# One tile for q and k of a head pair, wider scores matmuls, and part of VectorE's copies and of the gate's "+1" on GpSimd: an attention + gated FFN kernel on one Trainium2 core

## The chip, the cores and the metric

The kernel runs on one core of one Trainium2 chip. The core has five engines that run side by side, each through its own instructions in order: TensorE (PE in the profile; its weight loads are shown apart as PEld), VectorE (DVE), ScalarE (ACT), GpSimd (POOL) and SyncE (SP, which here only issues DMAs). The metric is the device time of one execution in microseconds (us); the number to predict is the median over runs. A profile is one execution with a record of every instruction.

## What is computed

Block-sparse attention (8 heads of 64, 4 batches, 768 tokens) and behind it a feed-forward network with a gate that is a convolution over three neighbouring tokens. In the reference's words, cut to what matters (B, H, S, D = 4, 8, 768, 64):

```python
scores = np.matmul(q, k.transpose(0, 1, 3, 2)) / np.sqrt(D)
...
scores = np.where(mask, scores, -1000000000.0)   # blocks of 32: window, edges, 3 sampled per row
attn = np.exp(scores - np.max(scores, axis=-1, keepdims=True))
attn = attn / (np.sum(attn, axis=-1, keepdims=True) + 1e-09)
x = np.matmul(attn, v).transpose(0, 2, 1, 3).reshape(B, S, H * D)
...
h = np.maximum(x @ w_in, 0.0)                    # 512 -> 1024
for k in range(3):
    conv_out += conv_w[k] * hp[:, k:k + S, :]    # hp: h with one zero row at each end
gate = 1.0 / (1.0 + np.exp(-conv_out))
out = (h * gate) @ w_out                         # 1024 -> 512
```

## The kernel before

The work is cut into 144 units of 1024 scores columns, in segments: half a batch (384 query tokens) each, the last half again in 256 + 128. Two heads form a pair; there are 16 pairs. A unit goes through this chain:

- *Scores* (L742, PE). For a 128-key block `kc` and a head, the stationary operand is k transposed, 88 rows: 64 of k and 24 rows that carry the block mask. The moving operand is q transposed with the mask's other factor in its 24 rows, so that the masked scores come out of one matmul. The result goes to a PSUM tile `st` of 1024 columns. There are two of these.
- *Exponential* (L753, ACT): one instruction for a unit, 128x1024, from `st` to `pt` in SBUF.
- *Attention times v* (L775, PE): eight matmuls of 65 columns for a unit; the 65th column of `V_t` is ones, so that the sums come along. DVE then takes reciprocals (L692) and normalises (L694), and the tokens are transposed into `xT`.
- *Feed-forward*: w_in matmuls (L864, PE), relu (L884 on ACT or L886 on DVE), the three-tap convolution as three DVE multiplies and two adds (L916, L924), tanh (L963, ACT), "+1" (L966, DVE), product with h (L971, DVE, to `gT`), w_out matmuls (L802, PE), copy from PSUM to `o2s` (helper lines L336 on ACT, L340 on DVE), output DMA (L809, SP).

q and k of a pair lie in two tiles, `E_t` and `O_t`, by the parity of the 128-token chunk: `E` has k chunks 0, 2, 4 and three of the six q chunks, `O` the rest. For pairs 0 to 5 they come from PE transposes (k: L466; q: L504, three 64-column ones for a head and half) and copies from PSUM; for pairs 6 to 15 from DMA transposes into `stg` and one DVE copy for each parity. The mask rows are made once in slot 0 and copied by DVE into the other four slots (`m_slot`, two copies of 1536 for each slot). v comes by DMA into `vn` and is copied into `V_t` with room for the ones column (`v_cp`, by DVE or ACT). The tap weights as diagonal matrices (`diag`, L387, DVE) serve the last segment, whose convolution is done on PE.

Since the q chunks of one half lie in both tiles, a scores matmul of one k block covers 128 or 256 columns (`blk_order`, `pieces`):

```python
blk_order = {0: [(0, 0, 0), (0, 1, 2), (1, 0, 1)], 1: [(1, 1, 0), (1, 2, 2), (0, 2, 1)]}
...
if pieces and pieces[-1][:4] == (P, hh, kc, par) and pieces[-1][4] + pieces[-1][6] == idx:
    pieces[-1] = pieces[-1][:6] + (pieces[-1][6] + 1,)
```

What sets the order: each piece of work is an `op` with the engines that may do it and a planned duration for each, its dependencies and buffers. A string, `ORDER`, written beforehand, lists all 1758 in one sequence with the engine and the buffer number of each; `put_down` walks it. So each engine's order is fixed, and an engine waits at an instruction whose data isn't there, with all behind it. Semaphores are placed by the framework, tile by tile.

POOL before: at the start it builds index tables (`affine_select`, L265 to L275), then it issues all loads of q, k, v and weights (L239, 65 of them), held back by 43 `pace` copies of one element (L414, L656), which only wait until an exponential or an earlier load is done.

The last two output blocks (`tail`) accumulate in the two halves of one `st` tile.

Of the kernel before, what the change touches and what calls it, by code (L numbers as in the profile page):

```python
# [8 lines left out]
BF16 = mybir.dt.bfloat16  # L9
# [23 lines left out]
i+18Y4i/2MV8/090j0Vj109158r2941958sj22Uj71960j3V9909a8Mjm0j409b12+9h1jo2/08t29i8Njnj89j2j58O0jp9m09nj9V8U0j6A8V
319r1jq9o3ja1jbju1jd0jvjrje8P9s9w0jcAjx8Z321308+92jfA93jwjj19t49xjC2jg0jhjyiZ9y5369E1js372jkjiV9798jz9cjE9F2u0jD
9d19G09J0jA9k9KjF9l9L19e19O1jt9p9q339PjlV9u2wA9T02vAjB9U9vk819Q2jK3k9jL9z9V3jGjY0393a29Y19f9A9ZjHjMa409g9H09IjN
9M9+4jZjOa59N9R8QjI9SjP9W3c9XjJa91aaa65kajQiT9/jRj+3bab09B2ae09Cj/2VV3af9Dk0A2kb3h2WVaj1ag1k20a11a2k33d0kcA3k4
2ZA3k5jS1k6V1a30jT34V4akjUal2ar0k1jVa01asjWA0ke0kfat3jXkh1kgV1kiaw135V3kkjAax3l3kn0ay4kokC03i0kk1kEaB0kpAklkDaC
kmAa7kFa8acaG1aD5kq0kGadaHkK1kt1kH3nahkMaL0kr3o13mkLaI0aikuksVamaMkvAkNkz03eaN1aT1kOaUkw1kS2ankPkx3skIkAao0kTaY0
aV2aZkJ1au0avazaAkyVaEkBAaFaJb11kVa+3b2aKkQl61apaOb34b60kRaqb7lc0kUb85be1k+3bfl7l03pbg0aP1kWaWbj0bkaQ2aXk/kXa/b0
b4bo1aRb5b9bl1bal1aSbh0bpldkYl2bq2bt0bikZbubmbb1l3lebcby1bzbv3bdl4bnl8l5brbsbA43qV0bG0bHk7l938V43fV1bI5lf3v3w1  # L40
laV2bL1bMlgA0bwbQ03rVli1bN0lh3gVljll0kdlkV3jA0lm3AbRlblnVbV1bWbS1lr1lG0lo0lIlsbX23x3B1lplHc10c2ltV3t1lqAbxc61lJ
c33c7bBbC1lO1lx1lylKc84cb0bJlzVcclD0lLlQcg1bKlP3ychlu1cd5bD0lRbObPlvbEbTci0lElMcl0bF1lSbUcmlwAbY3KlNct13L0lTlA1
lW2bZculYcn1c40lB3zlXc5c9calFVcv33Hcy03I2czb+2lUcelZlCAmg03PlVcA4cD1cfcEl+mh3Mb/cF2cjcI0ck3uV1ma1c0m23l/cJcom3
cp1cQ1cRcK5m4cw3CcxcBm5cCcGmbcS0m0m6cV0cHcLm1cM3NcWm7c+1cq1micrcX1c/m8mccscN0m9cT0cUd03d30cOd4mjcPd54cY3Zmd3+2
mkV1d81d9meV0mm03Q0da5dg03DV2mn3JV2mo3EV423OcZmfdhd1mpdi03W3Gdl1mqV3dmmy1dn1mz3/mB0mC3X0mAA0dq0mDVd2drms1mW0ds2
mtmX3Rdv1dwmYmudx3mZmE0mv40m+431d6d7mwV2mFm/dD0dbmGVdEdI1dc1n0dF4mH1n10mIdJdd2mJAmN04cde4d3dN0dK5mOn21df2dj41dO
n3dkmK1n4dP0mL494a1n5domxdpdS1dTmPVmMA4hdtdudX0dU13SV3dYdy3TVmQ1mRdZ2n6e314e4i0e4na2dzmT0nbe53mUmSVdG0e80dHe9n7
mVVdLed1dA1eeni3ea4nw1dBdMdQdRncdVef5dCdWd+ei04fndejnq0n8ek0e00eq1neer3Fd/1n9e6e744es1ev0njewnrnkex3eA1e1eb3VeB
ecnlege2nfehel4gem3YV3et0eF0nmeC4nx4ong4p2eueyen2eznheGnneK1eonyeH5eLepnonsnpeDeEeM045V4eS0eT4jnteU2eX1nuV0eYnz
eZ14bV4eI48eJnAV2eNf00mrf1eO1eP1f5146Vf23mlf6nC0eQ47nDf74nI1eR0nEVnJfd04qV0nKAfe4kV1nL0ff5nM3Ufi1nNVnvfjnF14lV  # L50
fk0eV4nnGo60eWnBfn0fonHAo8nR0fp2nSo7fs1n+1e+e/ftnTAn/nO1fu1nPo9fx0o0fyf3nQAf4o1nU0fz3fF1oafGf8f9o2nVfH4nX1oe2fg0
fK0offLo3nYogfhfP1fa0fM5flnZVfQfmfqo4frfbobfU0o5fvfcfVnWAohoA1fR0ocfwou0om3fAodfW2g01g1onfB1fIovoig21g50oog6oBop
ojfJfNfC2fOoqfSg73fTga1fDgbfXfYokfEg30org4g8olg9gj0gkgc4osoCotowgl5fZ1go1f+gpoxgq0f/gdoDoyV3gt0gugeoM0gv24mgf0oN
ggozoOoEA1oPoFgC1oQA0gDgh1gH0giA1gIoS0gE1oToV1oUV1gJ3oWgM1oXVgNp20gO4p3pe1p51pgp6p4Apfgm1gV0p7AgngrphoY0oZpigW
o+Agso/1pu0pjp0pwoG0pvp1Ag+1g/gX5oHpm2oIpnh00oJpogwh30pph4oKA2gxpxpb1h52gF0pqoLpcp80gy2pkoRgGpdAgKgzgLgPhc1prpy
hdgQpl1gY1gZhe1h1p9psh2gR1h6ptgA1hh0paAh7gShigBAhq1h80pC3hrhj3pK0pDgT1pLh9hs4gUVhf0hz0pFhgha1hkpzhl1hbVhApEhthu
pZ1hB5hv2pGp+hwhE1pHp/VhFhN0hC1hOpAhG0q31pIpBq4pJhDpMq5Aqe1hHpNhP2hJ1hm0pQ1qfhnpRpOA3qhpSqu2ho0qgpThpA2qwhI0pW0
pUA1hKqvpXpVqihL1hQhRpYAhMVpPhS0hx1hThyAq60qjhU0q01hVVq7qR0qSq8q1qTAq9qkq2AqO0qaqPqlr31qbqX1qQVqYr4qcq+0qZAqU0qd
qVq/qm3qC1qWAqor01qDqnr50qI0r1r6r80r2rd1qpri0qqr9rer7ro1qrqxrprf1qyra0qJqsqzqtrjqEqAqBqKrbqLrcrgqFrhqMA2rqqGV0qN
rrrkqHrsA1rlrtrmA3rn  # L60
# [52 lines left out]
def kernel(  # L113
# [23 lines left out]
    WHOLE = ()  # L137
    SEQ = "nq0 nq1 k4 q4 w0 v4 w1 nq2 w2 k5 q5 w3 v5 nq3 k6 q6 v6 k7 q7 v7 nq4 nq5"
# [16 lines left out]
    E_t = many(NSLOT, [88, 2, 2, 3, 128], BF16, "e")  # L155
    O_t = many(NSLOT, [88, 2, 2, 3, 128], BF16, "o")
# [145 lines left out]

    ECH, OCH = [(0, 0), (0, 2), (1, 1)], [(0, 1), (1, 0), (1, 2)]

    def w24(e):
        w = st_t[b_w.index]
        for x, chunks in enumerate((ECH, OCH)):
            for y, (g, c) in enumerate(chunks):
                nc.tensor.matmul(out=w[0:NB, 512 * x + 128 * y:512 * x + 128 * y + 128], lhsT=aadd,
                                 rhs=nblk[:, 384 * g:384 * g + 384].rearrange("j (p c) -> j c p", c=3)[:, c],  # L310
                                 start=True, stop=True)

    o_w = op("w24", {"PE": 0.34}, w24, -17, [o_a4, o_nblk], alloc=[b_w])

    def q_rows(dst, x):
        def fn(e):
            w = st_t[b_w.index][0:NB, 512 * x:512 * x + 384]
            to = dst[64:88, 0, 0].rearrange("p c s -> p (c s)")
            if e == "ACT":
                nc.scalar.copy(out=to, in_=w)  # L320
            else:
                nc.vector.tensor_copy(out=to, in_=w)
        return fn

    m_q = [op("m_q0", {"ACT": 0.45, "DVE": 0.55}, q_rows(E_t[0], 0), -17, [o_w], uses=[b_w]),
           op("m_q1", {"DVE": 0.55, "ACT": 0.45}, q_rows(O_t[0], 1), -17, [o_w], uses=[b_w])]

    def k_rows(dst, x):
        return lambda e: dcopy(e, dst[64:88, 1, 0], nblk.rearrange("j (p c t) -> j t c p", c=3, t=2)[:, x])

    m_k = [op("m_k", {"DVE": 0.6, "ACT": 0.5}, k_rows((E_t, O_t)[x][0], x), -13, [o_nblk]) for x in range(2)]
    mask_ready = {(0, 0): m_q + m_k}

# [12 lines left out]
    def wl(e):  # L346
        for y, (t0, c, n_) in enumerate(((384, 0, 2), (640, 0, 1), (384, 1, 2))):
# [7 lines left out]
    m_h1 = []  # L355
    for x, t in enumerate((E_t, O_t)):
        m_h1.append(op("m_h1", {"DVE": t_d4(768)}, lambda e, t=t: dcopy(e, t[0][64:88, :, 1], t[0][64:88, :, 0]),
                       T(0) + 0.1 * x, [m_q[x], m_k[x]]))
    mask_ready[(0, 1)] = m_h1
    for s in range(1, NSLOT):  # L360
        mr = []
        for x, t in enumerate((E_t, O_t)):
            mr.append(op("m_slot", {"DVE": t_d4(1536) + 0.05}, lambda e, t=t, s=s: dcopy(e, t[s][64:88], t[0][64:88]),
                         T(4.5 * s - 2.5) + 0.1 * x, [m_h1[x]], earliest=7.0 + 2 * s))
        mask_ready[(s, 0)] = mask_ready[(s, 1)] = mr
# [354 lines left out]
    for u, (n, blocks) in enumerate(units):  # L720
# [3 lines left out]
        for part in range(2):  # L724
            bls = blocks[4 * part:4 * part + 4]
            heads, pieces = [], []
            for x, (P, hh, kc, par, idx, c) in enumerate(bls):
                if (P, hh) not in heads:
                    heads.append((P, hh))
# [288 lines left out]
```

## Time and profile before

| what | us |
|---|---|
| runs | 217.66, 217.71, 220.73 |
| median | 217.71 |
| the profiled execution's own time | 215.81 |
| its span, first to last instruction | 213.9 |
| first exponential starts | 7.88 |
| last evicting copy ends | 210.9 |

The page gives for each engine the time in which at least one of its instructions was running (busy). Records of consecutive instructions overlap by their latency, so a busy engine need not be at its peak: for the rate, compare starts. The chain that ended last is followed back from the last instruction, at each step to what released it; its shares say on which engine time is on the path. A group's line reads: line, engine, operation, output<-inputs, shapes, count | busy us, mean ns of one | idle time before them and what ended it. A timeline's line: start, duration, engine, line, operation, tiles, shape, count [idle before <- releaser].

The TensorE clock was at its full value in the whole profile (PEclk 9, the highest digit, in all slices).

### The profile page before, as it was taken

The page shows a single profiled execution, that of the slowest core. Times are in us where ns is not written, and L with a number is a line of the kernel's source. Part 1 is how long each engine was busy: PE and PEld are TensorE (multiplying, and loading weights), DVE is VectorE, ACT ScalarE, POOL GpSimd, SP SyncE. Part 2 cuts the span into 40 slices and gives each one's busy share as a digit, 9 for nine tenths or more (in the row PEclk, how much of TensorE's full clock was granted, in tenths as well). Part 3 has the DMA queues.
Part 4 walks back from the last instruction along what each step waited for, and adds up shares of the span by engine and source line. Part 5 has one row for each costly group of instructions (what it writes and reads, how often), then busy time and mean ns, then how long its engine had stood idle before and what let it go on. Part 6 is the DMA issues. An engine that isn't in the chain of part 4 may idle for free.

```text
span 213.9 us, 6829 instructions
## 1 busy us (share of the span) xinstructions
PE 203.6 (95%) x2702; PEld 154.0 (72%) x2721; DVE 186.6 (87%) x577; ACT 193.5 (90%) x252; POOL 60.4 (28%) x117
## 2 busy tenths in 40 slices
PE   7899999999999999999999999999998999999991
PEld 3679978887677775778776766787786867785740
DVE  4899989999989994999999978999799939999980
ACT  6999999999899997999999977999999988997642
POOL 8883455733323130500327152730000000000000
PEclk9999999999999999999999999999999999999999
DMA  6999898998888977693599869699941130200205
GB/s 181 186 195 202 132 123 119 113 172 99 99 123 99 138 133 162 122 106 74 103 234 96 116 104 188 105 143 114 134 154 23 20 122 3 98 5 21 80 0 196
DMA packets 48935, 24.81 MB, mean 116 GB/s; under 512 B 35120, under 2 KB 45832, under 8 KB 48904
## 3 DMA queue, kind: packets, MB, share of 16 engines
q0 software_dynamic: 19728, 11.05, 43.0%
q1 hardware_dynamic: 28888, 13.05, 30.0%
q8 instruction: 21, 0.34, 0.7%
q10 hardware_dynamic: 288, 0.30, 0.4%
q14 instruction: 10, 0.08, 0.1%
HBM read 23.08 MB, written 6.29 MB: 137 GB/s over the span
## 4 chain that ended last, share of the span: by engine, by line
PE 66%; DVE 24%; ACT 6%; issue 3%; ACTq 0%; DVEq 0%
PE st L742 19%; PE mix L802 16%; PE mix L864 12%; PE av L775 10%; DVE m L916 9%; ACT pt L753 4%; DVE m L924 4%; DVE hE L886 3%; PE st L802 2%; PE mix L504 2%; PE av L230 2%; DVE xtok L694 1%; DVE gT L971 1%; DVE o L340 1%; DVE e L340 1%
## 5 line engine op out<-in xcount | busy, mean ns | idle before, releaser
L753 ACT ACTIVATE pt<-st 128x1024 bf16<-128x1024 f32 x144 | 141.3, 1027 | 5.6 <-PE st L742 4.2
L775 PE MATMUL av<-vt,pt 128*128 128x65 bf16 x1152 | 60.4, 193 | 0.2
L775 PEld LDWEIGHTS <-pt 128*128 128x128 bf16 x1152 | 52.3, 97 | 10.1
L864 PE MATMUL mix<-xT,winb 128*128 128x384 bf16 (+2 forms) x288 | 52.8, 308 | 0.3 <-DVE hE L886 0.3
L916 DVE TENSOR_SCALAR m<-hE,cw 128x382 bf16<-128x382 bf16 (+2 forms) x192 | 49.4, 320 | 0.2
L802 PE MATMUL mix<-woutb,gT 128*128 128x512 bf16 x157 | 44.6, 379 | 1.6 <-DVE gT L971 0.6
L742 PE MATMUL st<-o 88*128 88x128 bf16 (+1 forms) x240 | 44.5, 229 | 0.3 <-ACT pt L753 0.2
L742 PE MATMUL st<-o,e 88*128 88x128 bf16 (+1 forms) x228 | 44.2, 233 | 0.2 <-ACT pt L753 0.2
L742 PE MATMUL st<-e,o 88*128 88x128 bf16 (+1 forms) x224 | 42.5, 234 | 1.2 <-ACT pt L753 1.1
L742 PE MATMUL st<-e 88*128 88x128 bf16 (+1 forms) x208 | 41.8, 239 | 0.4 <-ACT pt L753 0.2
L742 PEld LDWEIGHTS <-o 88*128 88x128 bf16 x464 | 34.3, 97 | 8.9 <-issue 2.0
L742 PEld LDWEIGHTS <-e 88*128 88x128 bf16 x436 | 32.9, 97 | 9.0 <-issue 0.9
L924 DVE TENSOR_TENSOR m<-m 128x764 bf16<-128x764 bf16 (+2 forms) x64 | 33.8, 533 | 0.3
L864 PEld LDWEIGHTS <-winb 128*128 128x128 bf16 x288 | 24.2, 97 | 8.2 <-issue 0.8
L963 ACT ACTIVATE m<-m 128x764 bf16<-128x764 bf16 (+2 forms) x32 | 26.3, 821 | 1.9 <-DVE m L924 1.8
L414 POOL COPY pace<-pt 1x1 bf16<-1x1 bf16 x24 | 7.6, 315 | 58.9 <-ACT pt L753 58.8
L802 PEld LDWEIGHTS <-gT 128*128 128x128 bf16 x192 | 15.7, 97 | 11.7 <-DVE gT L971 2.3
L886 DVE TENSOR_SCALAR hE<-mix 128x384 bf16<-128x384 f32 (+2 forms) x30 | 16.4, 553 | 7.9 <-PE mix L864 7.6
L884 ACT ACTIVATE hE<-mix 128x384 bf16<-128x384 f32 (+2 forms) x34 | 16.5, 492 | 3.1 <-PE mix L864 2.2
L971 DVE TENSOR_TENSOR gT<-m,hE 128x764 bf16<-128x764 bf16 (+3 forms) x36 | 18.3, 511 | 0.5
L694 DVE TENSOR_TENSOR xtok<-av,rcp 128x384 bf16<-128x384 f32 (+2 forms) x36 | 18.2, 507 | 0.4
L239 POOL DMA_DIRECT2D nat<-in_q_dram x23 | 16.9, 734 | 2.4 <-issue 1.9
(88 smaller groups left out, 170.0 us busy)
## 6 DMA issues: line engine op xcount, KB each, us to landing
out_dram<-o2s SPq DMA_DIRECT2D x24, 256.0 KB, 2.6
nat<-in_k_dram POOLq DMA_DIRECT2D x15, 192.0 KB, 4.0
vn<-in_v_dram POOLq DMA_DIRECT2D x15, 192.0 KB, 5.5
nat<-in_q_dram POOLq DMA_DIRECT2D x6, 192.0 KB, 4.2
winb<-in_moe_w_in_dram POOLq DMA_DIRECT2D x2, 512.0 KB, 8.4
woutb<-in_moe_w_out_dram POOLq DMA_DIRECT2D x4, 256.0 KB, 4.8
nat<-in_q_dram POOLq DMA_DIRECT2D x9, 96.0 KB, 5.4
nq<-in_q_dram POOLq DMA_DIRECT2D x6, 96.0 KB, 4.5
```

Of the source, the lines that this page charges most:

```text
L239: return op(name, {eng: occ}, lambda e: on(e).dma_start(out=dst(), in_=src), prio, deps, dma=(kind, service), **kw)
L694: nm = op("norm", {"DVE": t_dps(128 * C)}, lambda e: nc.vector.tensor_tensor(out=xtok_t[xk.index][:, 0:C].rearrange("p c h d -> p h c d"), ...
L742: nc.tensor.matmul(out=st[:, 128 * x:128 * (x + n_)], lhsT=QK[kc % 2][s][0:88, 1, hh, kc // 2, :], rhs=QK[par][s][0:88, 0, hh, idx:idx + n ...
L753: nc.scalar.activation(out=pt_t[ptb.index], in_=st_t[stb.index], func=AF.Exp, bias=0.0, scale=0.125)
L775: nc.tensor.matmul(out=o[:, off:off + 65], lhsT=pt_t[ptb.index][:, 128 * x:128 * x + 128], rhs=V_t[vslot_b[P].index][:, hh, kc, 0:65], sta ...
L802: nc.tensor.matmul(out=acc(), lhsT=gT_t[gb.index][:, ffc, 128 * t:128 * t + 128], rhs=woutb[:, ffc, :], start=(ffc == 0), stop=(ffc == NFF ...
L864: nc.tensor.matmul(out=mix_t[hb.index][:, w1 * y:w1 * y + w1], lhsT=winb[:, fc, 128 * ffc:128 * ffc + 128], rhs=xT_t[xt_buf[n].index][:, f ...
L886: nc.vector.tensor_scalar(out=dst, in0=src, scalar1=0.5, scalar2=0.0, op0=ALU.mult, op1=ALU.max)
L916: nc.vector.tensor_scalar(out=m_t[cb.index][:, x, y, 0:w], in0=hE_t[heb.index][:, f0 + y, t0 + x:t0 + x + w], scalar1=cw[:, x, f0 + y:f0 + ...
L924: nc.vector.tensor_tensor(out=m[:, a_, :, 0:w], in0=m[:, a_, :, 0:w], in1=m[:, b_, :, 0:w], op=ALU.add)
L963: th = [op("tanh", {"ACT": t_act(2 * w) + 0.04}, lambda e, cb=cb, w=w: nc.scalar.activation(out=m_t[cb.index][:, 0, :, 0:w], in_=m_t[cb.in ...
L971: nc.vector.tensor_tensor(out=gT_t[gtb.index][:, f0:f0 + 2, t0:t1], in0=m_t[cb.index][:, 0, :, 0:w], in1=hE_t[heb.index][:, f0:f0 + 2, 1 + ...
```

## The change

- `F_t` replaces `E_t` and `O_t`: one tile a slot, with all six chunks of q and of k in order. The order of the chunks of a half is now 0, 1, 2, so that a scores matmul covers up to 384 columns, cut only where a 512-column PSUM bank ends. 900 scores matmuls become 600. Dependencies of a scores matmul are kept by half and by key parity.
- q is transposed with two PE instructions for a head and half (one of 128 columns, two chunks at once, and one of 64) instead of three.
- Copies into `F_t` write every other chunk; the mask is built half by half, and copied to another slot in one instruction of 3072 elements.
- The last output block of the last segment goes in two halves of 256 columns, each with its own PSUM region, copy and DMA.
- `POOL_ALT`: POOL becomes a possible engine for the v copies, for the mask copy into slots 3 and 4, for the diagonals and for the gate's "+1". `ORDER` is written anew; in it POOL does 9 of 16 v copies (DVE 4 and, for the first pair, 1 more; ACT 2), 1 of 4 slot copies, 5 of 8 diagonals and 18 of 36 "+1" (DVE before: all of the "+1", of the diagonals and of the slot copies, and 13 of the v copies). DVE's evictions of output blocks go from 11 to 7 whole ones and a half one, ACT's from 13 to 16 whole ones and a half one.

```diff
+    POOL_ALT = True
...
-    E_t = many(NSLOT, [88, 2, 2, 3, 128], BF16, "e")
-    O_t = many(NSLOT, [88, 2, 2, 3, 128], BF16, "o")
+    F_t = many(NSLOT, [88, 2, 2, 6, 128], BF16, "f")
...
-        for x, t in enumerate((E_t, O_t)):
-            mr.append(op("m_slot", {"DVE": t_d4(1536) + 0.05}, lambda e, t=t, s=s: dcopy(e, t[s][64:88], t[0][64:88]),
-                         T(4.5 * s - 2.5) + 0.1 * x, [m_h1[x]], earliest=7.0 + 2 * s))
+        mr = [op("m_slot", {"DVE": t_d4(3072) + 0.05, "POOL": 2.9} if POOL_ALT and s > 2 else {"DVE": t_d4(3072) + 0.05},
+                 lambda e, s=s: dcopy(e, F_t[s][64:88], first_f[64:88]), T(4.5 * s - 2.5), m_h1, earliest=7.0 + 2 * s)]
...
+            if e == "POOL":
+                nc.gpsimd.tensor_tensor(out=diag[:, :, f], in0=ident.unsqueeze(1).broadcast_to([128, 3, 128]),
+                                        in1=cw[:, :, f].unsqueeze(2).broadcast_to([128, 3, 128]), op=ALU.mult)
+                return
...
-                    for y, cc in enumerate((0, 2, 1)):
-                        pos = (2 * x + y) if y < 2 else 2 * w + x
-                        nc.tensor.transpose(out=t[0:64, 128 * pos:128 * pos + 128],
-                                            in_=src()[:, hh, 64 * cc:64 * cc + 64], identity=ident)
+                    nc.tensor.transpose(out=t[:, 256 * x:256 * x + 128], in_=src()[:, hh, 0:128], identity=ident)
+                    nc.tensor.transpose(out=t[0:64, 256 * x + 128:256 * x + 256], in_=src()[:, hh, 128:192],
+                                        identity=ident)
...
-        v_ready[P] = op("v_cp", {"DVE": t_d4(768) - 0.05, "ACT": t_act(768)},
+        v_ready[P] = op("v_cp", {"DVE": t_d4(768) - 0.05, "ACT": t_act(768), **({"POOL": 0.9} if POOL_ALT else {})},
...
-                if pieces and pieces[-1][:4] == (P, hh, kc, par) and pieces[-1][4] + pieces[-1][6] == idx:
-                    pieces[-1] = pieces[-1][:6] + (pieces[-1][6] + 1,)
+                if pieces and pieces[-1][:3] == (P, hh, kc) and pieces[-1][3] + pieces[-1][5] == idx:
+                    pieces[-1] = pieces[-1][:5] + (pieces[-1][5] + 1,)
...
-                    nc.tensor.matmul(out=st[:, 128 * x:128 * (x + n_)],
-                                     lhsT=QK[kc % 2][s][0:88, 1, hh, kc // 2, :],
-                                     rhs=QK[par][s][0:88, 0, hh, idx:idx + n_, :].rearrange("p c s -> p (c s)"),
+                    nc.tensor.matmul(out=st[:, 128 * x:128 * (x + n_)], lhsT=f[0:88, 1, hh, kc, :],
+                                     rhs=f[0:88, 0, hh, idx:idx + n_, :].rearrange("p c s -> p (c s)"),
...
+            def g1_fn(e, cb=cb, w=w):
+                t = m_t[cb.index][:, 0, :, 0:w]
+                if e == "POOL":
+                    nc.gpsimd.tensor_scalar(out=t, in0=t, scalar1=1.0, scalar2=1.0, op0=ALU.add, op1=ALU.mult)
+                else:
+                    nc.vector.tensor_scalar(out=t, in0=t, scalar1=1.0, scalar2=None, op0=ALU.add)
...
+            cuts = (0, DM // 2, DM) if lastn and t == 5 else (0, DM)
+            for x in range(len(cuts) - 1):
+                out_block(b, t, base + W * 0.75 + 0.12 * W * (t - tok // 128) + 0.5 * x, d, [] if lastn else rl_all,
+                          lastn, cuts[x], cuts[x + 1])
```

`dcopy` copies on the engine it is given (ACT, POOL or DVE).

More of the change, by code (lines that the diff above doesn't have):

```diff
@@ L668 @@
     units = []
-    for n, (b, g, _, C, order) in enumerate(SEGS):
+    for n, (b, g, _, C, c0) in enumerate(SEGS):
         blocks = []
@@ L771, in a_fn @@
                 o = av_t[ab.index]
[L772 removed]
+                for y, (P, hh, kc, idx, c) in enumerate(bls):
                     x = 4 * part + y
```

243 lines of the change are left out of this document (119 added, 124 removed).

## The prediction

> **What bounds the kernel now.** I read the page first: busy shares, then the chain that ended last. Three engines are close to full, and the chain is mostly TensorE's, a quarter VectorE's.
>
> ```profile
> span 213.9 us, 6829 instructions
> PE 203.6 (95%) x2702; PEld 154.0 (72%) x2721; DVE 186.6 (87%) x577; ACT 193.5 (90%) x252; POOL 60.4 (28%) x117
> ...
> PE 66%; DVE 24%; ACT 6%; issue 3%; ACTq 0%; DVEq 0%
> ```
>
> The busy times by stretch say that the middle has no spare engine: from 60 to 80 us and from 100 to 120 us DVE, ACT and PE are all over 96%. Only POOL has room.
>
> ```profile
> 60.00:80.00 20.00, 19.71 (x262) 15.05 (x262) 19.27 (x57) 19.84 (x27) 5.62 (x11) 1.00 0.84 123
> 100.00:120.00 20.00, 19.58 (x263) 14.87 (x262) 19.52 (x57) 19.88 (x25) 7.90 (x14) 1.00 0.86 137
> ```
>
> The timeline of PE shows what a matmul really costs. A record lasts 0.22 us, but the next one starts 0.06 us later (two 128-wide ones) or 0.11 us later (behind a 256-wide one): PE is paced by columns, and the weight loads lie under them.
>
> ```profile
> 100.06 0.22 PE L742 MATMUL st<-e,o 88*128 88x128 bf16 x1
> 100.12 0.22 PE L742 MATMUL st<-o 88*128 88x128 bf16 x1
> 100.18 0.27 PE L742 MATMUL st<-e,o 88*128 88x256 bf16 x1
> 100.29 0.28 PE L775 MATMUL av<-vt,pt 128*128 128x65 bf16 x4
> ```
>
> The timelines of POOL and DVE show that these two stop each other. A one-element POOL copy takes 0.18 us beside a DVE instruction that reads PSUM (L886), and 0.61 us beside one that reads two SBUF tiles (L924): it ends 0.05 us after that one. The other way round, a DVE multiply (L916, 0.32 us as a rule) that starts 0.16 us after a POOL DMA issue takes 0.61 us and ends 0.06 us after the issue.
>
> ```profile
> 105.23 0.56 DVE L886 TENSOR_SCALAR hE<-mix 128x384 bf16<-128x384 f32 x1
> 105.60 0.18 POOL L414 COPY pace<-pt 1x1 bf16<-1x1 bf16 x1 [1.11 <-ACT pt L753]
> ...
> 51.38 0.61 POOL L414 COPY pace<-pt 1x1 bf16<-1x1 bf16 x1 [3.87 <-ACT pt L753]
> 51.39 0.55 DVE L924 TENSOR_TENSOR m<-m 128x764 bf16<-128x764 bf16 x1
> ...
> 52.85 0.71 POOL L239 DMA_DIRECT2D nq<-in_q_dram  x1
> 53.01 0.61 DVE L916 TENSOR_SCALAR m<-hE,cw 128x382 bf16<-128x382 bf16 x1
> ```
>
> The tail's timeline: PE's last two matmuls wait 0.72 us for ACT's copy out of the other half of the same PSUM tile, then the last copy takes 0.59 us.
>
> ```profile
> 209.05 0.59 ACT L336 COPY o2s<-st 128x512 f32<-128x512 f32 x1 [1.19 <-PE st L802]
> 209.69 0.59 PE L802 MATMUL st<-woutb,gT 128*128 128x512 bf16 x2 [0.72 <-ACT o2s L336]
> 210.31 0.59 ACT L336 COPY o2s<-st 128x512 f32<-128x512 f32 x1 [0.68 <-PE st L802]
> ```
>
> Rows by shape, for prices (busy, mean):
>
> ```profile
> L265 POOL TENSOR_SCALAR_AFFINE_SELECT ident<-ident 128x128 bf16<-128x128 bf16 x1 | 0.3, 294 | 0.0
> L269 POOL TENSOR_SCALAR_AFFINE_SELECT A<-A 24x24 f32<-24x24 f32 x1 | 0.2, 197 | 0.0
> L966 DVE TENSOR_SCALAR m<-m 128x764 bf16<-128x764 bf16 x16 | 5.7, 359 | 0.3 <-ACT m L963 0.2
> L340 DVE COPY vt<-vn 128x768 bf16<-128x768 bf16 x12 | 4.1, 346 | 0.1
> ```
>
> **Base.** The sum is made against the profiled execution: span 213.9 us, time 215.81, so 1.9 us lie outside the span. The median of three runs, 217.71, is another 1.9 us above it. I carry both over unchanged and forecast the median.
>
> **The change, part by part.** Counts are those of the two built programs' instructions.
>
> *Wider scores matmuls.* 648 of 128 columns and 252 of 256 become 216 of 128, 216 of 256 and 168 of 384: 900 to 600. At the starts' pitch (0.055, 0.109; 0.162 for 384, from L864, where eight take 1.30 us): 63.1 becomes 62.6 us, -0.5. The 300 weight loads that go (97 ns each) were under the matmuls, so nothing for them; if that cover were not whole, the gain would be larger, never smaller. Bounds: -0.5 and -2.
>
> *Fewer turns.* q needs two transposes a head instead of three: 72 to 48, 24 x 0.056 = -1.3 us of PE, before about 60 us. The two copies behind them keep their sizes.
>
> PE carries 66% of the chain, so of these 1.8 us I take 1.2.
>
> *Start.* The first scores need only the even half of k and the first half of the mask rows. Before, ACT reaches the first exponential at 7.88 us, behind three copies from 6.74 us on, one of them for the second head. In the new order ACT stands ahead of it with a cast of the second q half (which landed at about 5.35 us: DVE starts its cast of it then), two mask copies and two short copies: 5.35 + 0.35 + 0.4 + 0.25 + 0.4 + 0.4 = 7.2 us. -0.6; bounds 0 (DVE's mask chain now stands behind a cast) and -0.9.
>
> *Tail.* The last block goes in two halves to two PSUM tiles. In the new order no matmul stands behind a copy of its own tile: -0.7. The last copy is 256 wide, 0.39 us by ACT's 128x256 row (L884) instead of 0.59: -0.2. Eight more matmuls cost 8 x 2 ns. The last DMA carries half; I take nothing for that. -0.9; bounds -0.2 and -1.4.
>
> *ACT.* Four more evictions of 512 (+2.4 us) against fewer small copies (about -2.4): nothing.
>
> *Work taken off DVE.* 8 of 12 v copies (0.346) -2.8; 18 of 36 "+1" (0.36; three shorter) -6.2; 15 diag products (4.4/24) -2.7; mask slots 8 x 0.56 to 3 x 1.0 (768 elements 0.35, 1536 0.56) -1.5; o2s 11 of 0.69 to 7 and a half one -2.3; more q, k and cast copies +0.5: -15 in records, and about -13 by starts, since DVE records overlap by some 0.07 us.
>
> *Put on POOL.* 33 instructions whose length no row shows. From the two affine rows: 97 ns for 104 elements, 0.93 ns each, so 764 elements take 0.197 + 0.69 = 0.89. 9 copies, 15 long and 3 short "+1" give 23; the mask slot (3072) 3.0; five diag products of 384 with two inputs 0.53 to 0.9, say 0.7: 3.5. Together 29.5 us; POOL goes from 60 to 90 of 214, it has room.
>
> *What that costs DVE.* Bounded from below by no conflict (0) and from above by all of it (29.5). Of the DVE instructions that stand next in order behind each POOL one, 15 of the 27 "+1"s and v copies have a multiply, add, copy or gate product of SBUF tiles right behind: those wait about 0.6 (0.89 less a mean 0.3 already gone). The rest have a PSUM reader (relu, normalisation, transposed copies) first, 0 to 0.5 each. With 2.5 for the mask slot: 9 + 3.5 + 2.5 = 15 us. I take 15, by the L916 and pace rows above. Net for DVE: +2, where -13 was to be had. At DVE's 24% of the chain: +0.5.
>
> *The "+1" in the gate's path.* ACT's tanh, "+1", then the product, which DVE meets in order with all behind it, and then the output matmuls. The "+1" takes 0.89 plus a wait for DVE's instruction at hand (pace rows: 0 to 0.43) instead of 0.36, so 0.55 to 1.0 later. The product stands three to five DVE instructions behind, some 1.8 us, which covers most; I take 0.2 for each of 18, 3.6 us of DVE waits, 24%: +0.9. If the cover is gone: 18 x 0.8 x 24% = +3.5.
>
> *Queues.* In POOL's queue DMA issues now stand behind copies that wait: behind the first v copy (its load is the third issued) the next loads, and behind it the mask slot and a diag product stand ahead of the second w_in load, issued at 14.08 us before. It goes out up to 5 us later and lands (8.4 us) at 27.5 us; the first output group that reads it is the fifth of segment 0, at about 33 us, since the first starts at 28.6 us. Hidden with 5 us to spare: 0, bound +2. SP loses four of eight small mask DMAs and gains two half outputs for one: 0.
>
> **Sum.** -1.2 - 0.6 - 0.9 + 0.5 + 0.9 = -1.3: profiled time 214.5, median **216.4 us**. Its own range: 214 to 219.
>
> **Rivals.**
>
> *Relief holds.* POOL's instructions fall mostly beside PSUM readers, as the 19 of 43 pace copies that took 177 to 189 ns. DVE gains 13 us, 24% on the chain: -3.1; all of PE's -1.8 counts; start -0.6, tail -0.9: -6.4, **211.3 us**. For it: every "+1" is placed several instructions ahead of its product. Against: the kind that conflicts (L916 49.4, L924 33.8, L971 18.3, "+1" 12, SBUF copies 15) is 128 of DVE's 187 busy us.
>
> *The port decides (slower).* Each POOL instruction holds DVE for its whole length. DVE gets +29.5 - 13 = +16.5, at 24% +4.0; the products come late, +3.5; less 2.7 for PE, start and tail: +4.8, **222.5 us**. It decides where DVE has no slack: 60 to 80 us leaves 0.73 us in 20, and three "+1"s there that cost 0.9 each use more. Against: PSUM readers go through, and POOL sometimes loses instead.
>
> [...]
>
> *The layout does nothing.* The wide matmuls are paced by columns, start and tail are eaten by later waits, POOL's effects cancel: 217.7. This lies within the forecast's band.
>
> **Chances.** Near balance (forecast, with the third rival) 0.56; relief 0.27; port 0.17. About 2% (4.35 us: under 213.4, over 222.1) is what a measurement of this kernel can tell from no change. Relief at 211.3 is faster, with a little of the forecast's lower edge lost to "same": faster 0.27, same 0.56, slower 0.17. For 8 in 10 the range reaches to both rivals' times: 211 to 222.
>
> **What will show it.** Starts of 384-wide matmuls 0.162 us apart; the first exponential near 7.2 us; no PE wait for o2s in the tail; POOL "+1" records of 0.9 us or more; L916 and L924 records of up to 1 us beside them; DVE busy near 188 us (relief: 174; port: 200). I am wrong if POOL's elements cost far more than 0.93 ns, or if DVE waits for POOL turn up at the products.

## The result, and the profile after

| | before | changed |
|---|---|---|
| runs, us | 216.45 to 220.73, median 217.69 | 232.18, 233.63, 233.69, 239.59, median 233.66 |
| ratio to before, 95% interval | | 1.077 (1.072 to 1.082) |
| profiled execution: time, span | 215.81, 213.9 | 233.63, 231.9 |
| first exponential starts | 7.88 | 8.62 |
| last exponential starts | 193.89 | 212.93 |

The forecast was 216.4, and -1.3 us against before; the change costs 16. Single runs of most versions, of the kernel before too, scatter by 3 to 7 us; the ratios leave disturbed runs out, and the experiments show where much of that scatter comes from.

The profile of the changed kernel, its span, busy times and the chain that ended last:

```profile
span 231.9 us, 6214 instructions
PE 215.2 (93%) x2405; PEld 147.4 (64%) x2405; DVE 189.6 (82%) x531; ACT 196.3 (85%) x253; POOL 93.2 (40%) x150
...
PE 42%; DVE 40%; ACT 9%; issue 5%; DMA 1%; ACTq 0%; DVEq 0%
```

DVE's share of the chain has gone from 24 to 40%, though it is busy for 3 us more only. Where the time is lost is best seen by a marker that both kernels have, the start of the k-th exponential. The changed kernel is behind by 0.7 us at the first, 7.1 at unit 12, 8.0 at unit 18, 11.4 at unit 63, 14.5 at unit 90, 19.0 at unit 143 (the last), and 18.0 at the end of the span. Three things can be read directly.

*The q transposes.* PE's timeline of the changed kernel, one pair of heads:

```profile
25.85 0.22 PE L498 MATMUL mix<-ident,nat 128*128 128x128 bf16 x1
26.00 0.24 PE L499 MATMUL mix<-ident,nat 128*64 128x128 bf16 x1
26.17 0.23 PE L498 MATMUL mix<-ident,nat 128*128 128x128 bf16 x1
26.33 0.24 PE L499 MATMUL mix<-ident,nat 128*64 128x128 bf16 x1
```

Compare starts, not durations: 0.15 to 0.18 us apart, where 128 columns behind each other take 0.055. Each step changes the stationary operand from 128 columns (128\*128) to 64 (128\*64) or back. Over all such steps of this profile at full clock the medians are 0.155 and 0.176, so a change takes some 0.11 us.

*The clock.* The first eight scores matmuls of the changed kernel, and of a run of it whose clock rose earlier (the seventeenth experiment, full clock from 5.2 us):

```profile
7.54 1.89 PE L732 MATMUL st<-f 88*128 88x384 bf16 x8
```
```profile
6.98 1.22 PE L732 MATMUL st<-f 88*128 88x384 bf16 x8
```

The same eight last 1.89 us in one and 1.22 in the other. In the changed kernel's profile PE runs at half clock until 24.3 us; in the profile of before until 5.7 us. The page's PEclk row shows 9 in all slices for both, since the trace has no record of the clock ahead of its first change: the clock of the start must be read from the distance of starts. So the clock of before was not full in its whole profile: its warm-up matmuls of 512 columns start 0.43 us apart, where 512 columns take 0.215 later.

*POOL beside DVE.* The timelines of DVE and of POOL around 102 us:

```profile
101.78 2.06 DVE L917 TENSOR_TENSOR m<-m 128x764 bf16<-128x764 bf16 x1
```
```profile
101.81 0.84 POOL L962 TENSOR_SCALAR m<-m 128x764 bf16<-128x764 bf16 x1
102.59 0.82 POOL L326 COPY vt<-vn 128x768 bf16<-128x768 bf16 x1
```

The add takes 0.55 us as a rule, here 2.06: it ends behind the second of two POOL instructions. A normalisation, which reads PSUM, keeps its 0.56 though it lies wholly beside a POOL instruction:

```profile
111.92 0.56 DVE L686 TENSOR_TENSOR xtok<-av,rcp 128x384 bf16<-128x384 f32 x1
```
```profile
111.28 1.19 POOL L962 TENSOR_SCALAR m<-m 128x764 bf16<-128x764 bf16 x1 [4.39 <-ACT m L956]
```

Six normalisations of this shape lie mostly beside a long POOL instruction; their median is 0.55, as that of the other 22. By shape, DVE and POOL of the changed kernel have (busy, mean ns of one):

```profile
L909 DVE TENSOR_SCALAR m<-hE,cw 128x386 bf16<-128x386 bf16 x72 | 22.1, 368 | 0.1
L917 DVE TENSOR_TENSOR m<-m 128x764 bf16<-128x764 bf16 x32 | 20.0, 629 | 0.3
```
```profile
L962 POOL TENSOR_SCALAR m<-m 128x772 bf16<-128x772 bf16 x9 | 9.1, 1016 | 27.9 <-ACT m L956 27.9
L379 POOL TENSOR_TENSOR diag<-ident,cw 128x384 bf16<-128x384 bf16 x5 | 4.3, 863 | 6.9 <-DVE cw L371 6.9
```

Before, the first two had means of 327 and 546:

```profile
L916 DVE TENSOR_SCALAR m<-hE,cw 128x386 bf16<-128x386 bf16 x72 | 18.9, 327 | 0.1
L924 DVE TENSOR_TENSOR m<-m 128x764 bf16<-128x764 bf16 x32 | 17.3, 546 | 0.2
```

Summed over all DVE records, what lies above the median that the same operation and shape had before (counting those over 60 ns) is 15.7 us in the changed kernel and 3.0 in the one before (8 records of the changed kernel have a shape that before has not, and are left out): POOL stretches DVE by 12.7 us. Below, "stretch" is this excess over that of before.

The tail came out as planned. ACT's last two copies in the changed kernel's timeline:

```profile
227.65 0.58 ACT L324 COPY o2s<-st 128x512 f32<-128x512 f32 x1 [1.22 <-DVE o2s L328]
228.51 0.37 ACT L324 COPY o2s<-st 128x256 f32<-128x256 f32 x1 [0.27 <-DMA out_dram<-o2s]
```

From the start of the last exponential to the end of the span it takes 19.0 us instead of 20.0.

### The profile page after: what moved, and what is told of

It reads as the page before. It is cut to its first block, busy times and chain, and to the rows that moved or that the text cites. A ratio compares the mean times of both kernels' runs of the same rounds, so it can differ in the third digit from the quotient of the medians.

```text
span 231.9 us, 6214 instructions
## 1 busy us (share of the span) xinstructions
PE 215.2 (93%) x2405; PEld 147.4 (64%) x2405; DVE 189.6 (82%) x531; ACT 196.3 (85%) x253; POOL 93.2 (40%) x150
## 4 chain that ended last, share of the span: by engine, by line
PE 42%; DVE 40%; ACT 9%; issue 5%; DMA 1%; ACTq 0%; DVEq 0%
DVE m L909 15%; PE st L732 13%; PE mix L794 10%; DVE m L917 8%; ACT pt L742 8%; PE mix L857 7%; PE av L764 5%; DVE f L328 4%; DVE gT L969 3%; DVE xtok L686 3%; DVE hE L879 3%; PE av L230 2%; PE mix L499 2%; DMA out_dram<-o2s 1%; PE mix L498 1%
## 5 line engine op out<-in xcount | busy, mean ns | idle before, releaser
L732 PE MATMUL st<-f 88*128 88x256 bf16 (+2 forms) x600 | 98.3, 278 | 0.6
L732 PEld LDWEIGHTS <-f 88*128 88x128 bf16 x600 | 49.4, 100 | 21.3 <-issue 3.5
L909 DVE TENSOR_SCALAR m<-hE,cw 128x382 bf16<-128x382 bf16 (+2 forms) x192 | 54.9, 346 | 0.6 <-ACT hE L877 0.4
L794 PE MATMUL mix<-woutb,gT 128*128 128x512 bf16 x176 | 47.7, 379 | 7.5 <-DVE gT L969 4.2
L962 POOL TENSOR_SCALAR m<-m 128x772 bf16<-128x772 bf16 (+3 forms) x18 | 17.9, 996 | 64.9 <-ACT m L956 62.0
L917 DVE TENSOR_TENSOR m<-m 128x764 bf16<-128x764 bf16 (+2 forms) x64 | 38.7, 606 | 0.5
L879 DVE TENSOR_SCALAR hE<-mix 128x384 bf16<-128x384 f32 (+1 forms) x29 | 16.0, 556 | 15.7 <-PE mix L857 15.4
L328 DVE COPY f<-mix 64x256 bf16<-64x256 bf16 (+3 forms) x31 | 12.7, 415 | 6.8 <-PE mix L499 2.4
L324 ACT COPY o2s<-mix 128x512 f32<-128x512 f32 x15 | 8.8, 588 | 4.8 <-PE mix L794 4.7
L328 DVE COPY f<-stg 64x1536 bf16<-64x1536 bf16 x20 | 11.8, 592 | 0.2
```

What stands on the lines that cost most here:

```text
L328: nc.vector.tensor_copy(out=dst, in_=src)
L732: nc.tensor.matmul(out=st[:, 128 * x:128 * (x + n_)], lhsT=f[0:88, 1, hh, kc, :], rhs=f[0:88, 0, hh, idx:idx + n_, :].rearrange("p c s -> ...
L794: nc.tensor.matmul(out=acc(), lhsT=gT_t[gb.index][:, ffc, 128 * t:128 * t + 128], rhs=woutb[:, ffc, c0:c1], start=(ffc == 0), stop=(ffc == ...
L879: nc.vector.tensor_scalar(out=dst, in0=src, scalar1=0.5, scalar2=0.0, op0=ALU.mult, op1=ALU.max)
L909: nc.vector.tensor_scalar(out=m_t[cb.index][:, x, y, 0:w], in0=hE_t[heb.index][:, f0 + y, t0 + x:t0 + x + w], scalar1=cw[:, x, f0 + y:f0 + ...
L917: nc.vector.tensor_tensor(out=m[:, a_, :, 0:w], in0=m[:, a_, :, 0:w], in1=m[:, b_, :, 0:w], op=ALU.add)
```

## The experiments

First theory: three costs add up, the width changes of the q transposes, the late full clock, and POOL against DVE. Rivals: POOL alone, the layout alone, the clock by chance. Medians below stand beside the median of the kernel before on the same chip; "lag" is the start of an exponential less its start in the profile of before.

**1. Transposes of one width.** In the changed kernel:

```diff
-nc.tensor.transpose(out=t[0:64, 256 * x + 128:256 * x + 256], in_=src()[:, hh, 128:192], identity=ident)
+nc.tensor.transpose(out=t[:, 256 * x + 128:256 * x + 256], in_=src()[:, hh, 64:192], identity=ident)
```

Chunk 2 then lies in rows 64 to 127, beside chunk 1 of the first transpose, and the copies take it from there.

> The changed kernel with one edit: the second transpose of each head and half of q takes 128 columns (64 to 191) instead of 64, so that no q transpose uses a 64-column stationary operand between two of 128; the copies behind it read the other rows. Theory (three costs add up: width switches on PE, a late full clock, POOL against DVE): the trace of the changed kernel has 0.16 and 0.18 us per q transpose where 0.056 was expected, 48 of them, so 5 us of PE go, and if the thin matmul stream of the start is also what keeps the clock at half until 24 us, another 4 to 7 go: 222 to 229 us, first full clock before 10 us. Rival POOL alone: 233 us, pitch of the transposes changes and nothing else. Rival layout alone (POOL costs nothing): about 217 us. Rival clock by chance: 229 us, with the clock rising at any time.

229.35 (before 217.13): just above the theory's range, and the time that the rival "clock by chance" gives, so the median doesn't part these two. The transposes start 0.06 us apart:

```profile
5.69 0.23 PE L498 MATMUL mix<-ident,nat 128*128 128x128 bf16 x1
5.75 0.22 PE L499 MATMUL mix<-ident,nat 128*128 128x128 bf16 x1
```

The profile has full clock from 5.3 to 8.7 us and again from 12.1; its lag at unit 18 is 3.3 us instead of 8.0. 4.3 us of 16 are the width changes and the clock together; POOL alone and the layout alone are both out.

**2 and 3. Nothing moved to POOL; and both edits.** In `ORDER` the 33 pieces of work of POOL go to DVE, each "+1" to the place just ahead of its product (as sequence):

```diff
-tanh, g1 on POOL, ..., g2 on DVE
+tanh, ..., g1 on DVE, g2 on DVE
```

> The changed kernel with all copies, diagonals and +1 that POOL had back on DVE, each +1 just ahead of its product; layout as in the change. Theory (three costs): the lag behind the kernel before grew from 8 us at unit 18 to 19 us at unit 143, that growth goes and the start stays: 222 to 225 us. Rival POOL alone: 216 to 218 us. Rival layout alone: 233 us or more, since DVE has 13 us more to do.

228.89. A miss: 4.8 us come back, not 9 to 12. Its clock is late as well, half from 12.1 to 22.4 us.

> Both edits at once: full-width q transposes and nothing of the moved work on POOL. Theory (three costs): all three gone, the wider scores matmuls, fewer turns and the tail are left: 213 to 218 us. Rival POOL alone: the same as without POOL, 216 to 218. If the layout itself costs (strided copies, the mask chain): above 220 us.

223.62, a miss too: 10.1 us come back, and 6.5 stay lost that none of the three costs explains. Its clock was full from 5.5 us on.

**4. POOL's part in the kernel before.** `v_cp`, `m_slot`, `diag` and "+1" get POOL as an engine, and as many of them as in the change are given to it in the old order, each "+1" right behind its tanh:

```diff
-g1 = op("g1", {"DVE": t_d4(2 * w) - 0.05}, ...
+g1 = op("g1", {"DVE": t_d4(2 * w) - 0.05, "POOL": 1.0}, ...
```

> The kernel before with only the POOL part: 9 v copies, one slot's mask copies, 5 diagonals and 18 of the +1 on POOL, each +1 right behind its tanh in the order. Theory (three costs): the POOL share of the loss alone, +8 to +11 us: 226 to 229 us. Rival POOL alone: the whole loss, 232 to 235 us. Rival layout alone: 216 to 219 us.

226.1 (before 217.13; ratio 1.038, 1.025 to 1.051): as the theory said, +9. The stretch is 13.5 us. The profile's lag is 2.6 us at unit 9 and 9.2 at unit 143; the clock was half once more from 14.2 to 17.6 us, which is part of the 2.6 but not all of it (the eighth experiment, at full clock from 4.0 us on, has 1.1 there).

**5. The layout in the old order.**

```diff
-    E_t = many(NSLOT, [88, 2, 2, 3, 128], BF16, "e")
-    O_t = many(NSLOT, [88, 2, 2, 3, 128], BF16, "o")
+    F_t = many(NSLOT, [88, 2, 2, 6, 128], BF16, "f")   # E_t is F_t[..., 0:6:2, :], O_t is F_t[..., 1:6:2, :]
```

> The kernel before, in its own order and with its own engines, with one edit: q and k in one tile, so that the scores matmuls are the wider ones of the change (no 64-column transposes between, nothing on POOL, old tail). What is left of the loss without POOL work and with wide transposes is 6.5 us (223.6 against 217.1). Theory (that rest belongs to the new order of the work, which was planned for a VectorE relieved by POOL, not to the layout): 215.5 to 218 us. Rival (strided copies and the merged tile cost): 220 to 224 us.

216.09, 220.53, 220.62 and 220.89, median 220.57 (before 216.94): by the median this is the rival's range. The profile, however, of the last of these, has half clock until 20.8 us; its lag is 5.3 us from unit 9 on and 5.1 at unit 143. So the layout costs nothing behind the start (it gains 0.2), the 5 us are lost in the start under the half clock, and the other 6.5 us are not the layout's. The eleventh experiment has the same layout and 216.75.

**7 to 9. Why POOL costs 9.** New theory: the "+1" comes late, and DVE, in order, waits with it. Rival: contention, which the recorded texts call the port: that is my name for whatever DVE and POOL stop each other at; the runs show how long the records last, not what is shared. The seventh experiment has the fourth's "+1" alone, the eighth the rest alone, the ninth this:

```diff
+ nc.gpsimd.tensor_scalar(out=scr[:, :, 0:w], in0=m_t[cb.index][:, 1, :, 0:w], scalar1=1.0, scalar2=1.0,
+                         op0=ALU.add, op1=ALU.mult)      # 17 of them; scr is read by nobody
```

> The kernel before with only 18 of the 36 +1 on POOL, each right behind its tanh in the order. Theory (a late +1 holds the product, behind it DVE in order, then the output matmuls): most of the 9 us that the whole POOL part cost the kernel before, 222 to 226 us. Rival (only the shared port counts): by POOL time, 18 of 27 us, half of it given back by DVE relief: 218 to 221 us.

> The kernel before with only 9 v copies, one slot's mask copies and 5 diagonals on POOL. Theory (late +1): 216 to 219 us, the port conflict and the relief of DVE about cancel. Rival (port, and POOL's queue of loads held up behind copies): 220 to 224 us.

> The kernel before with all its work where it was, and 17 extra POOL instructions of the length of the +1 that nobody waits for: they read the sum that goes into the tanh and write a scratch tile, in the places where the POOL +1 stood. Contention alone, with no lateness and no relief. Theory (late +1 is the main cost, contention costs DVE 6 to 9 us of records of which a third reaches the end): 218 to 221 us. Rival (contention is the main cost): 223 to 227 us. No conflict: 217 us.

Only "+1": 220.73; only copies, mask and diagonals: 221.39; dummies: 225.41 (before 216.94; ratio of the dummies 1.038, 1.028 to 1.049). All three are where the rival put them, and the theory of the late "+1" falls: POOL work that nobody waits for and that relieves nobody costs 8.5 us. The rows of the ninth:

```profile
L972 POOL TENSOR_SCALAR scr<-m 128x772 bf16<-128x772 bf16 x9 | 8.3, 921 | 30.1 <-DVE m L925 29.9
```
```profile
L917 DVE TENSOR_SCALAR m<-hE,cw 128x386 bf16<-128x386 bf16 x72 | 23.3, 388 | 0.1
```

The stretch is 9.7 us, the lag at unit 143 is 9.4. The seventh has nearly the same POOL instructions, and DVE is relieved of the "+1": its stretch is 7.3 us, and from unit 18 to 143 its lag grows by 3.0. For the eighth these are 7.6 and 3.3, for the fourth 13.5 and 6.6. So relief that comes together with stretch gives back about half of it.

**10. Relief alone.**

```diff
+gs = [o for o in gr.ops if o.name == "g1"]
+for x in (4, 5, 6, 8, 9, 10, 12, 13, 14, 20, 21, 22, 24, 25, 26, 29, 31, 33):
+    gs[x].fn = None
```

> The kernel before with the 18 +1 that the change gave to POOL left out altogether (part of the gate is not computed): VectorE is relieved of 18 instructions of 0.36 us, 6.2 us by starts, and nothing is added anywhere. The price of VectorE time when it is taken away. By its 24% of the chain, as the prediction had it: -1.5 us, 215.5. If VectorE bounds the kernel one to one: -6 us, 211. If relief of one of three full engines brings next to nothing while a delay of it counts in full (the dummy run: 9.7 us of longer records, 8.5 us of time): 0 to -1 us, 216 to 217.

Median 219.24 (before 217.86), ratio 0.995 (0.988 to 1.001). In the profile the lag goes from +0.2 to -0.6. So 6.2 us less work for DVE, with nothing else changed, bring under 1 us in the profile; the interval of the runs reaches to 2.5, so it rules out one to one but not the 1.5 by the share. The chain is PE's:

```profile
PE 68%; DVE 15%; ACT 11%; issue 3%; DMA 1%; SPq 0%; ACTq 0%
```

**14 and 15. Conflict or queue.** The dummy kernel again, with one element, and with half the columns:

```diff
-out=scr[:, :, 0:w], in0=m_t[cb.index][:, 1, :, 0:w]
+out=scr[0:1, 0:1, 0:1], in0=m_t[cb.index][0:1, 1, 0:1, 0:1]      # fourteenth
+out=scr[:, :, 0:w // 2], in0=m_t[cb.index][:, 1, :, 0:w // 2]    # fifteenth
```

> As the dummy run (e9_before_dummy, 225.41 us), but each of the 17 extra POOL instructions handles one element instead of 128 x 772: POOL's queue still waits for the same sums, so its loads go out as late, but the port is hardly used. Theory now (the port: a POOL instruction stretches VectorE's records, and what VectorE loses reaches the end one to one): 216.5 to 218.5 us. Rival (loads held up in POOL's queue): 223 to 226 us.

> As the dummy run, with half the columns in each of the 17 extra POOL instructions, so that they last half as long. Theory now (port for the length of the instruction): half of the 8.5 us, 220 to 222 us. Rival (a fixed price for each POOL instruction): 224 to 226 us; rival (queue): 223 to 226 us.

One element: 216.48, 216.83, 220.84, 220.88, median 218.83 (before 218.01), between the two forecasts; the profile, of the last, has half clock until 20.0 us, and from there its lag only grows from 4.8 to 5.2. Half length: 220.17, ratio 1.013 (1.008 to 1.018), lag 3.2 at unit 143.

```profile
L972 POOL TENSOR_SCALAR scr<-m 1x1 bf16<-1x1 bf16 x17 | 4.7, 277 | 74.0 <-DVE m L925 64.7 <-DVE rcp L691 9.1
```
```profile
L972 POOL TENSOR_SCALAR scr<-m 128x386 bf16<-128x386 bf16 x9 | 5.7, 633 | 29.0 <-DVE m L925 28.8
```
```profile
L917 DVE TENSOR_SCALAR m<-hE,cw 128x386 bf16<-128x386 bf16 x72 | 20.6, 349 | 0.1
```

| 17 extra POOL instructions | stretch, us | lag gained from unit 18 to 143, us |
|---|---|---|
| 1 element | 0.8 | 0.4 |
| half length | 4.2 | 2.9 |
| full length | 9.7 | 9.4 |

POOL waits for the same sums in all three (74, 73 and 74 us), so the queue is out: it is the conflict, by its length, and of what DVE loses 0.7 (half length) to nearly all (full length) reaches the end.

**11. Layout and wide transposes in the old order**, nothing on POOL, the last output block in a PSUM tile of its own (the edits of the fifth and the first, and in `ORDER`):

```diff
-f2 of one of the last two blocks: tail 1
+f2 of one of the last two blocks: tail 2
```

> The kernel before in its own order and with its own engines, with q and k in one tile (wide scores matmuls), two full-width transposes for a head and half of q instead of three, and the last output block in a PSUM tile of its own; nothing on POOL. Theory (the 6.5 us left without POOL work and width switches are the new order's): 214.5 to 216.5 us where the clock comes up early. Rival (fewer transposes or the layout cost in the start): 219 to 223.

216.75 (215.4 to 218.6; before 217.86), ratio 0.999 (0.994 to 1.004). The same layout as in the third experiment, 7 us faster, and just above the range that was expected. The third's lag goes from 0.9 us at unit 45 to 9.1 at unit 143; this one's stays between 0.9 and 1.5 from unit 18 on. Waits of the third and of this one (who waits, for whom: us in total, times, longest):

```profile
DVE hE L878 <- PE mix L856: 15.2, 10, 4.3
PEld L793 <- DVE gT L968: 7.8, 14, 1.4
```
```profile
DVE hE L880 <- PE mix L858: 7.0, 6, 2.8
...
PEld L796 <- DVE gT L965: 3.2, 10, 0.5
```

In the new sequence PE reaches output matmuls before DVE has made their products, and waits 7.8 us for them instead of 3.2; DVE waits 15.2 us instead of 7.0 for w_in matmuls. That the second wait comes of the first is read from the order, not shown by a run.

**16. The sequence or the split.** The third experiment with 9 evictions changed between ACT and DVE, nearly as before dealt them (11 of 24 on DVE there; engines in `ORDER`):

```diff
-ev on DVE: 8 of 25
+ev on DVE: 13 of 25
```

> The run with full-width transposes and nothing on POOL (e3_wide_no_pool, 223.6 us), with the copies out of PSUM of the output blocks dealt to ACT and VectorE as in the kernel before (12 of the first 22 on VectorE instead of 6), in the new order otherwise. The 6.5 us that are left there: if the new split between ACT and VectorE makes them: 217 to 220 us. If it is the sequence itself (matmuls of an output block set before their products are done): 223 to 227 us, PE still waiting some 7 us for the gate's products.

224.04, and PE waits for the products as long as there:

```profile
PEld L793 <- DVE gT L968: 7.8, 14, 1.4
```

So it is not that split. The sequence is what is left; which of its places cost how much was not tried. The copies of the mask, the dependencies of a scores matmul and the halves of the last output block differ too between the third and the eleventh; the mask copies belong to the start and the halves to the end, while the third's loss lies between.

**12, 13 and 17. The clock.** Second theory of the clock, an estimate of mine from the profiles so far: how busy PE is ahead of a change decides it. The changes lay 3.4 us or a multiple of it apart (5.3, 8.7 and 12.1 us in the first experiment, 12.1 and 22.4 in the second, 14.2 and 17.6 in the fourth). The twelfth adds to the eleventh, the thirteenth takes from the kernel before:

```diff
+for x in range(3):      # behind w24, the first q_tr, the second k_tr
+    op("warm", {"PE": 0.1}, lambda e: nc.tensor.matmul(out=av_t[1][:, 0:256], lhsT=warm[:, 0:128], rhs=warm[:, 0:256], ...
...
+for o in [o for o in gr.ops if o.name == "warm"][5:10]:
+    o.fn = None
```

> The same as e11_before_layout_turns with three more matmuls of 256 columns on the warm-up tile, between the first transposes. [...] If the extra matmuls only delay: +0.3 us and the same scatter.

216.49 (215.27 to 219.01; before 217.86); ratio 0.994 (0.989 to 0.998). The theory's forecast was no run with a late clock. Of before 15 of 35 runs lie above 218.9, here 1 of 12; but of the eleventh, without the three matmuls, it is 0 of 12, at 216.75. So the runs don't show that the three matmuls do anything, and the late clock was not kept away: the profile has full clock from 4.1 us, half again from 11.0 to 17.8.

> The kernel before with five of its first ten warm-up matmuls left out. [...]

220.12 (217.4 to 221.78; before 217.86); ratio 1.005 (0.999 to 1.012). The theory's forecast, 220 to 222 us with a late clock in every run, is a miss in part: the runs begin at 217.4, and the profile has full clock from 11.9 us and a lag of 2.3. The 3.41 us ahead of that hold 11 transposes, which have 128 rows, so it seems that these count. As a measure of how busy PE is, take the time in which columns are fed (0.83 us for 1000 at half clock, by the warm-up matmuls, and half of that at full clock) times rows/128, as a share of an interval of 3.41 us; call it the rows share. Some intervals, counted from a change of the clock:

| profile | interval, us | rows share | clock in it, after it |
|---|---|---|---|
| changed | 0.44 to 3.85 | 0.76 | half, half |
| changed | 7.27 to 10.68 | 0.70 | half, half |
| changed | 20.92 to 24.33 | 0.78 | half, full |
| before | 2.28 to 5.69 | 0.78 | half, full |
| thirteenth | 8.45 to 11.86 | 0.77 | half, full |
| second | 8.70 to 12.12 | 0.36 | full, half |
| third | 5.48 to 8.89 | 0.41 | full, full |

> The changed kernel itself once more. If the late clock of its profile (24.3 us) was one throw among others: another time of the rise in this profile, and single times that spread by 5 us or more with it. If it is a fixed property of the change: again 24 us after the start, and times within 1 us of 233.7.

232.06, 232.72, 234.08, 237.96, median 233.4; full clock from 5.2 to 8.6 us and again from 18.8. So it is a throw in part; how often the changed kernel wins it, two profiles don't tell. A clock once lost stayed lost for some 10 us here (8.6 to 18.8) and in the second experiment (12.1 to 22.4), which also has the narrow transposes, and for 3.4 in the first (8.7 to 12.1), which has wide ones; that the narrow ones are the reason was not shown. The second's busy times by stretch (the third column from the end is PEclk):

```profile
5.00:12.00 7.00, 6.06 (x50) 3.56 (x49) 6.18 (x21) 5.86 (x10) 6.11 (x9) 1.00 1.30 188
12.00:22.00 10.00, 10.00 (x81) 6.82 (x80) 7.04 (x15) 5.60 (x7) 6.27 (x11) 0.51 1.31 202
```

From 12 to 22 us PE is busy all the time, at half speed, while DVE has work for 7.0 us of 10 and ACT for 5.6.

## Why the prediction was wrong, point by point

Three steps failed. The order of the work was put at nothing, without a reason; the new order costs 7 to 8 us by itself. What POOL does to DVE was put at +0.5, by netting relief against stretch and weighing the rest by DVE's 24% of the chain; it costs 6.6 us in the old order. And the q transposes, put at -1.3 with the clock taken as full, cost some 4 to 5 with the late clock that goes with them. Term by term:

- *Scores matmuls, -0.5:* 0.2 seen, in the lag of one profile (experiment 5), which is too little to tell from nothing.
- *Fewer turns, -1.3:* failed, and in sign. Priced at 0.056 us each, but the two kinds alternate, and 24 pairs take 0.155 + 0.176 instead of 0.111: 5.3 us more. The trace of before had the price: from a 64-column transpose to the start of a 128-column one behind it, 0.15. I looked at starts of one kind only.

```profile
6.00 0.22 PE L504 MATMUL mix<-ident,nat 128*64 128x128 bf16 x1
6.15 0.23 PE L466 MATMUL av<-ident,nat 128*128 128x128 bf16 x1
```

- *Start, -0.6, first exponential at 7.2:* 7.69 in the third experiment, 8.62 in the profile with the half clock. ACT's chain was right in order, but the copies wait for PE and DVE in between. That the clock could be half there was not in my sum at all; it costs 2 to 5 us in experiments 5, 13 and 14, and here about 7 at unit 12 together with the width changes.
- *Tail, -0.9:* right, -1.0.
- *POOL's prices:* 29.5 us forecast, 32.8 measured (93.2 less 60.4); 1.02 for a "+1" of 772 columns instead of 0.89.
- *DVE's wait, 15 us:* about right, 12.7.
- *"At DVE's 24% of the chain: +0.5":* this step failed. I netted relief against stretch and weighed the rest by a share. Taken singly, the two have different prices: 6.2 us of relief bring under 1 us in the profile (experiment 10), 9.7 us of stretch cost 9.4 (experiment 9). DVE, ACT and PE are all over 96% busy in the middle, as I had quoted: that the next engine holds where one is relieved, and that nothing gives where one is delayed, would explain it. Together they have neither price. In the fourth experiment 13.5 us of stretch, with some 12 of relief at the prediction's prices, cost 6.6 us behind unit 18: the net of 1 to 2 is far too little even at one to one, and the stretch at one to one with relief at nothing is twice too much. Experiments 7 and 8 say the same. My rival "the port decides" had the direction and the same wrong weight, so it stopped at 222.5.
- *The late "+1", +0.9:* no more than that; no wait of a product for POOL is among the large ones, and dummies that delay nothing cost as much.
- *Queues, 0:* right as far as was tried (experiment 14, in the old order).
- *Not in the sum:* the new sequence. I worked out the operations and took the order of the work for neutral; with POOL's work back and transposes of one width 6.5 us stay lost (experiment 3), which the old order doesn't lose (experiment 11).

By differences of medians POOL takes 4.8, width changes and their clock 4.3, both together 10.1, and the 6.5 are what is left, so this sum proves nothing. The lag is a better measure, since the start and its clock drop out of it behind unit 18. Gained from unit 18 to unit 143, in us, with the experiments:

| | old order | new order |
|---|---|---|
| POOL's part not moved | -0.2 to 0.5 (5, 11, 12, 13) | 7.0 to 7.9 (2, 3, 16) |
| POOL's part moved | 6.6 (4) | 10.3 to 11.8 (1, 17, the changed kernel) |

So the new order costs 7 to 8 us without POOL's part and 4 to 5 beside it, and POOL's part costs 6.6 in the old order and 3 to 4 in the new one. That they don't add up fits a sequence planned for the relief; that was not shown. The rest of the changed kernel's loss, 8.0 us at unit 18, falls to 3.3 with wide transposes and an earlier clock (experiment 1), and the tail gives back 1.0.

## What to carry to other kernels

A share of the chain doesn't price a change of load: where three engines are full, what one loses may count nearly one to one (9.4 of 9.7 us here), and what it gains next to nothing by itself (under 1 of 6.2). Where both come in one change, the truth lay between here, at about half of the loss (6.6 of 13.5); take the two as bounds, until a run shows more. Look for two shapes that alternate on PE, and price the change between them by the start-to-start time of unlike neighbours (here 0.155 and 0.176 us, against 0.055 for like ones). When work is written into a fixed order, the order is part of the change: compare waits of the products, not only counts.

## What was not expected of the hardware

- In the profiles that show more than one change of the clock here, the changes lie 3.4 us or a multiple of it apart: 5.3, 8.7 and 12.1 us (experiment 1), 12.1 and 22.4 (2), 14.2 and 17.6 (4), 4.1, 11.0 and 17.8 (12), 5.2, 8.6 and 18.8 (17). How busy PE was ahead of a rise: of the eight intervals of 3.41 us at half clock in the profiles of before and of the changed kernel, counted back from the rise, the two with a rows share of 0.78 were followed by full clock, the six with 0.59 to 0.76 were not; the thirteenth's 0.77 was. From full clock the second's 0.36 lost it, the third's 0.41 kept it. These are too few, and lie too close, for a threshold. Columns without the factor for rows don't part them: 0.97 stayed at half (changed, 7.27 to 10.68 us), 0.93 rose (before, 2.28 to 5.69). Rows padded to 128 were not tried.
- The measure parts these intervals only with the transposes counted as work: without them the one ahead of the rise of before has 0.73, and the changed kernel's from 0.44 to 3.85 us, which stayed at half clock, 0.76.
- A change between a 128- and a 64-column stationary operand took some 0.11 us of PE in the changed kernel (0.155 and 0.176 from start to start, instead of 0.055). One between 88 and 128 rows cost nothing that shows: in the profile of before a matmul of the other kind starts 0.055 us behind one of 128 columns.
- A POOL instruction on 128 x 772 bf16 took 0.92 (experiment 9) to 1.02 us (the changed kernel) in the mean, on 128 x 386 0.63 (experiment 15), with two inputs on 128 x 384 0.86 (the changed kernel).
